# Weight scales from norms, scores in float16 halves, a layer function as a maximum, and four pairs' memory steps together

## Chip, cores and metric

The kernel runs on one core of one Trainium2 chip. The metric is the device time of one execution in microseconds (us). Engines are named as in the profile: PE (TensorE matmul) and PEld (its weight loads), DVE (VectorE), ACT (ScalarE), POOL (GpSimd) and SP, which here only issues DMAs.

## The reference

Causal attention over 4 batches of 8 heads, 576 positions and width 64, mixed by a gate with a memory term, feeds two dense layers in a row. All inputs are float32.

```python
scores = scale * np.matmul(q, k.transpose(0, 1, 3, 2))      # causal mask, softmax -> a
local = np.matmul(a, v)
q_p = phi(q)
mem_out = einsum(q_p, M_prev) / (einsum(q_p, z_prev) + 1e-6)
x = g * mem_out + (1 - g) * local                           # -> (2304, 512)
h = x @ w_in
g = np.where(h >= 1, h, np.where(h <= -1, 0.0, (h + 1) ** 2 / 4))
y = g @ w_out                                               # first layer
h = y @ w_in2
g = np.maximum(h, 0.0) + alpha * np.minimum(h, 0.0)
out = g @ w_out2                                            # second layer
```

The weights arrive as float64 (512 x 2048 and 2048 x 512 in each layer).

## The kernel before

**Products.** A dense product is made of float16 halves: every operand is scaled by a power of two and split into a high and a low half (`copy` writes the high one, `rest` the difference), and `mm_in` and `mm_out` add three products, high by high, high by low and low by high. Each of the four dense products is 1536 matmuls of 128 x 128 weights by 288 columns; the profile names them h<-x,w1i (first layer in), y<-g,w1o (first layer out), h<-yt,w2i and o<-g,w2o.

**Weights.** `Weights.groups` (called as w1i0 to w1i3, w1o0 to 3, w2i0 to 3, w2o0 to 3) loads the float64 bits of two groups of weights, takes the absolute maximum of each raw piece on DVE (16 pieces of 512 columns for each weight), brings the maxima together over the partitions in `all_max` (a PE transpose, a DVE maximum, a PE product with ones), makes a scale from the exponent, builds each group's values in a tile t (tag wt, two buffers; ACT and DVE), and then writes the halves with `copy` and `rest`. `scales1` needs the scale of every group of w1i. The halves of w2o lie in the tag wa, where w1i's lie until the first layer has used them.

**Attention.** `prepare` (p0 to p3, one for each batch) loads q, z, v and M, computes phi(q) and the memory's norms pair by pair, and makes the batch's scales from maxima. `scale_memory` multiplies q by the norms. `attend` handles two heads (a pair) at a time in five blocks of query rows with 64, 192, 320, 448 and 576 key columns. A block's scores are two matmuls at once, one for each head on 64 of the 128 rows of PE (s<-qk, float32, which the profile shows as two instructions each; the last block is done as 288 + 288 columns). DVE reads the scores from PSUM with the mask and the maximum (CUSTOM_DVE_ANT_0, e<-s,mask), ACT takes the exponential, and ACT, DVE and POOL scale them into p. Batch 0 (`PLAIN`, sections a0A and a0B, four pairs each) goes on in float32 with PE transposes; batches 1 to 3 (a1C to a3C, twelve pairs) use float16 halves, a DMA transpose (pt<-p) and float16 products (px<-pt,vh).

**First layer's function.** `up1` makes 2 x 288 columns of h at a time in PSUM (tag f, two buffers), ACT writes u and d from it, `shift` adds a constant to d on one of three engines, DVE multiplies the two, and `split` makes the halves g. There are 64 such steps.

**Order.** `Plan` records every operation, with the engines that may run it (`plan.either`), and orders them beforehand by a list of priorities of small pieces of the program (`RANK`) and a table of chosen engines (`HOME`), with costs and a limited number of buffers of each tag. The instructions are then issued engine by engine in that order, and every queue runs in order. Of PSUM's eight banks, the tag s (scores, and the products of `all_max`) has two, px two, and f two tiles of two. All engine instructions are recorded in one helper, so all have the line 424 in the profile.

## Time and profile before

| what | us |
|---|---|
| median of three runs (1044.55 to 1045.64) | 1044.62 |
| the profiled execution, its own time | 1042.5 |
| the profiled execution, first to last instruction (span) | 1040.6 |
| busy: PE / PEld | 947.1 / 709.2 |
| busy: DVE / ACT / POOL | 684.7 / 515.6 / 375.7 |

The mean granted clock of PE is 0.993 of 2.4 GHz. Busy times are sums over a span whose stages have different limits, so they are read by stage. A matmul's duration includes its way through the pipeline (286 ns for 288 columns), so the cost of one in a stream is the distance from one start to the next. A wait is put down to what came last before the instruction started.

### The profile page before, as it was taken

To read this page: it belongs to the slowest core of one execution; us is meant where nothing else is said; L and a number is where in the kernel's file an instruction comes from. 1 tells how busy PE (TensorE), PEld (TensorE's weight loads), DVE (VectorE), ACT (ScalarE), POOL (GpSimd) and SP (SyncE) were. 2 spreads that over 40 slices of the span, in tenths; PEclk is the share of its full clock that TensorE was granted. 3 is DMA by queue.
4 is the path that set the end of the run, shared out by engine and by line. 5 is a ranking of instruction groups with operands and counts; after the bars stand their busy time and mean duration, and the time that the engine had idled before them with its cause. 6 is when DMAs were issued, how large, how long until landed. Compare 5 with 4: busy or idle time off the path is not lost.

```text
span 1040.6 us, 20570 instructions
## 1 busy us (share of the span) xinstructions
PE 947.1 (91%) x8043; PEld 709.2 (68%) x8043; DVE 684.7 (66%) x1803; ACT 515.6 (50%) x1030; POOL 375.7 (36%) x405
## 2 busy tenths in 40 slices
PE   2178779999999999999989999999999999999998
PEld 1156446666667666766667777777777777777776
DVE  6979989989887788987877889892323413042320
ACT  5458777667566663765456646332322423131220
POOL 1353554667466673543533521251010111100020
PEclk9999988999999999999999999999999999999999
DMA  9833324567755774376654152320001000000000
GB/s 334 291 113 122 135 89 135 129 133 184 164 126 112 162 164 94 71 157 124 118 145 146 48 171 82 129 86 24 30 18 35 12 13 12 24 1 23 7 18 23
DMA packets 132096, 104.23 MB, mean 100 GB/s; under 512 B 98464, under 2 KB 113312, under 8 KB 132000
## 3 DMA queue, kind: packets, MB, share of 16 engines
q1 hardware_dynamic: 132000, 102.93, 36.9%
q8 instruction: 63, 1.03, 0.4%
q14 instruction: 33, 0.27, 0.1%
HBM read 66.73 MB, written 9.44 MB: 73 GB/s over the span
## 4 chain that ended last, share of the span: by engine, by line
PE 40%; DVE 4%; DMA 3%; POOL 2%; issue 2%; ACT 1%; SPq 0%; ACTq 0%; POOLq 0%
PE h L424 21%; PE o L424 17%; PE y L424 3%; DMA pt<-p 1%; DMA w2o_raw<-in_w2o 1%; DVE u L424 1%; DMA w2i_raw<-in_w2i 1%; POOL d L424 1%; POOL w2o L424 0%; DVE p L424 0%; ACT u L424 0%; DVE yt L424 0%; DMA yr<-y 0%; POOL p L424 0%; ACT d L424 0%
## 5 line engine op out<-in xcount | busy, mean ns | idle before, releaser
L424 PE MATMUL y<-g,w1o 128*128 128x288 f16 x1536 | 203.7, 286 | 1.8 <-DVE g L424 1.5
L424 PE MATMUL h<-x,w1i 128*128 128x288 f16 x1536 | 200.5, 286 | 4.6 <-ACT d L424 2.1
L424 PE MATMUL h<-yt,w2i 128*128 128x288 f16 x1536 | 194.8, 286 | 1.3 <-ACT u L424 1.3
L424 PE MATMUL o<-g,w2o 128*128 128x288 f16 x1536 | 193.9, 286 | 0.5 <-POOL w2o L424 0.5
L424 DVE SCALAR_TENSOR_TENSOR u<-u,al 128x288 f32<-128x288 f32 x128 | 67.0, 555 | 186.8 <-ACT u L424 186.6
L424 PEld LDWEIGHTS <-w1i 128*128 128x128 f16 x1536 | 146.9, 98 | 50.9 <-issue 12.7
L424 PEld LDWEIGHTS <-w1o 128*128 128x128 f16 x1536 | 145.0, 98 | 51.3 <-issue 12.6
L424 PEld LDWEIGHTS <-w2i 128*128 128x128 f16 x1536 | 150.1, 98 | 39.3 <-issue 1.5
L424 PEld LDWEIGHTS <-w2o 128*128 128x128 f16 x1536 | 150.1, 98 | 38.6 <-POOL w2o L424 0.8
L424 POOL TENSOR_TENSOR g<-u,g 128x576 f16<-128x576 f32 x54 | 74.1, 1372 | 182.7 <-ACT g L424 132.6
L424 ACT ACTIVATE e<-e,mxt 128x576 f32<-128x576 f32 (+4 forms) x160 | 88.3, 553 | 65.6 <-DVE mxt L424 55.1
L424 ACT ACTIVATE u<-h,sa 128x288 f32<-128x288 f32 x128 | 58.5, 498 | 125.5 <-PE h L424 122.3
L424 POOL TENSOR_SCALAR g<-u 128x576 f16<-128x576 f32 x40 | 30.5, 764 | 213.4 <-DVE u L424 156.9
L424 PE MATMUL s<-qk 64*128 64x288 f32 (+4 forms) x384 | 89.7, 481 | 15.8 <-DVE mxt L424 14.2
L424 DVE TENSOR_TENSOR g<-u,g 128x576 f16<-128x576 f32 x74 | 59.9, 810 | 31.5 <-ACT g L424 18.7
L424 ACT ACTIVATE oe<-o,osc 128x288 f32<-128x288 f32 x32 | 16.0, 501 | 111.4 <-PE o L424 111.4
L424 DVE SCALAR_TENSOR_TENSOR u<-u,c,d 128x576 f32<-128x576 f32 x64 | 59.7, 934 | 14.4 <-POOL d L424 10.1
L424 DVE CUSTOM_DVE_ANT_0 e<-s,mask 128x288 f32<-128x288 f32 (+4 forms) x160 | 64.3, 419 | 6.6 <-PE s L424 4.2
L424 PEld LDWEIGHTS s<-qk 64*128 64x128 f32 x384 | 40.0, 203 | 42.0 <-DVE mxt L424 27.4
L424 ACT ACTIVATE u<-h,bu,su 128x576 f32<-128x576 f32 x64 | 52.8, 825 | 21.8 <-PE h L424 16.6
L424 ACT ACTIVATE g<-u 128x576 f16<-128x576 f32 x61 | 41.6, 681 | 43.8 <-DVE u L424 23.2
L424 DVE SCALAR_TENSOR_TENSOR p<-e,sm,p 128x320 f16<-128x320 f32 (+4 forms) x80 | 57.0, 730 | 8.2 <-POOL p L424 5.8
(221 smaller groups left out, 1247.4 us busy)
## 6 DMA issues: line engine op xcount, KB each, us to landing
ring<-in_w1i SPq DMA_DIRECT2D x16, 512.0 KB, 6.2
w1o_raw<-in_w1o SPq DMA_DIRECT2D x16, 512.0 KB, 3.7
w2i_raw<-in_w2i SPq DMA_DIRECT2D x16, 512.0 KB, 3.8
w2o_raw<-in_w2o SPq DMA_DIRECT2D x16, 512.0 KB, 3.8
qk<-in_qk SPq DMA_DIRECT2D x12, 576.0 KB, 4.6
qn<-in_qn SPq DMA_DIRECT2D x16, 320.0 KB, 3.4
vc<-in_vc SPq DMA_DIRECT2D x16, 320.0 KB, 4.3
y<-ye SPq DMA_DIRECT2D x32, 144.0 KB, 2.5
```

Source lines behind the costliest of these rows:

```text
L424: fn(*args, **kw)
```

## The change

The scales of w1i, w1o and w2o no longer come from maxima of the raw pieces but from norms: ACT squares the finished tile t (into the place of the group's own high half), PE sums the squares with ones, and DVE makes the exponent (`root_exponent`), group by group; for w1i the squares of each column are summed, for the others those of the whole group. w2i keeps its maxima. In `prepare` ACT sums squares of v and M, and for batches 1 to 3 also sums |k| and the negative part of q; the operations on the norms run once for the four pairs. In `attend`, batches 1 to 3 load q and k raw into tag tmp (three buffers), split them into float16 halves, and make the scores as three float16 products; blocks 0 and 1 share a run, an exponent step, a p tile and a DMA transpose. In `up1` DVE limits h from PSUM, ACT squares it, and DVE takes the larger of that and the scaled h from PSUM. `shift` is gone. `RANK` and `HOME` are replaced throughout; their lists are left out here.

```diff
+    ROOT = 2.04**0.5
+    def root_exponent(twice, name):
+        top = tiny.tile([P, 1], F32, tag="p2m1", name=f"{name}_ret")
+        f = tiny.tile([P, 1], I32, tag="p2e1", name=f"{name}_ref")
+        V.tensor_scalar(out=top, in0=twice, scalar1=2.0**-118, scalar2=2.0**118, op0=ALU.max, op1=ALU.min)
+        V.tensor_scalar(out=f, in0=top.bitcast(I32), scalar1=24, scalar2=None, op0=ALU.logical_shift_right)
+        return f
...
-    ones = const.tile([8, P], F32, name="ones")
+    ones = const.tile([P, P], F32, name="ones")
+    ones16 = ones.bitcast(BF16).rearrange("p (n t) -> p n t", t=2)[:, :, 1]
...
-                    V.tensor_reduce(
-                        out=mx[:, k, i : i + 1],
-                        in_=raw[:, :, 1].bitcast(F32),
-                        axis=AX,
-                        op=ALU.max,
-                        apply_absolute_value=True,
+                    if self.bound is None:
+                        V.tensor_reduce(
+                            out=mx[:, k, i : i + 1],
+                            in_=raw[:, :, 1].bitcast(F32),
+                            axis=AX,
+                            op=ALU.max,
+                            apply_absolute_value=True,
+                        )
...
+                    plan.part(f"m{k}")
+                    sk = self.scale(g, tv, hi)
                 plan.part(f"s{k}")
-                copy(hi, tv, s[:, k : k + 1], (A, V, G))
-                rest(lo, tv, s[:, k : k + 1], hi, (G, V))
+                copy(hi, tv, sk, (A, V, G))
+                rest(lo, tv, sk, hi, (G, V))
+        def scale(self, g, t, hi):
+            name = f"{self.name}{g}"
+            squares = hi.bitcast(BF16)
+            pb = psum.tile([P, 512], F32, tag="s", name=f"{name}_pb")
+            if self.bound == "column":
+                A.activation(out=squares, in_=t, func=AF.Square, scale=ROOT)
+                by_block = squares.rearrange("p (f k c) -> p f k c", f=2, k=KK)
+                with plan.one():
+                    for kk in range(KK):
+                        T.matmul(
+                            pb[:, : 2 * P].rearrange("p (f c) -> p f c", f=2),
+                            lhsT=ones16,
+                            rhs=by_block[:, :, kk],
+                            start=kk == 0,
+                            stop=kk == KK - 1,
+                        )
+                n2 = tiny.tile([P, 1], F32, tag="wmg", name=f"{name}_n2")
+                V.tensor_reduce(out=n2, in_=pb[:, : 2 * P], axis=AX, op=ALU.max)
+                dst, of = self.inv[:, g : g + 1], slice(0, P)
+            else:
+                sq = tiny.tile([P, 1], F32, tag="wmx", name=f"{name}_sq")
+                A.activation(out=squares, in_=t, func=AF.Square, scale=ROOT, accum_out=sq)
+                T.matmul(pb[:, 0:1], lhsT=ones, rhs=sq, start=True, stop=True)
+                n2 = pb[:, 0:1]
+                of = slice(64 * (g % 2), 64 * (g % 2) + 64)
+                dst = self.inv[of, g // 2 : g // 2 + 1]
+            f = root_exponent(n2, name)
+            s = tiny.tile([P, 1], F32, tag="ws", name=f"{name}_s")
+            V.tensor_scalar(
+                out=s.bitcast(I32), in0=f, scalar1=float(-ONE23), scalar2=float(205 * ONE23), op0=ALU.mult, op1=ALU.add
+            )
+            V.tensor_scalar(
+                out=dst.bitcast(I32), in0=f[of], scalar1=float(ONE23), scalar2=float(49 * ONE23), op0=ALU.mult, op1=ALU.add
+            )
+            return s
...
-        rns = []
+        rn = tiny.tile([P, NPAIR, NB, 2], F32, tag="rn", name=f"rn{b}")
         for i in range(4):
             t = buf([P, 640], F32, "tmp", f"vc{b}_{i}")
             Q.dma_start(out=t, in_=vc[b, i])
-            V.tensor_reduce(out=mx[:, i : i + 1], in_=t, axis=AX, op=ALU.max, apply_absolute_value=True)
+            A.activation(out=t, in_=t, func=AF.Square, scale=ROOT, accum_out=mx[:, i : i + 1])
...
+            if halved:
+                t = buf([P, S], F32, "tmp", f"kc{b}_{pr}")
+                Q.dma_start(out=t, in_=qk[b, pr, :, 1])
+                A.activation(out=t, in_=t, func=AF.Prelu, alpha=-1.0, accum_out=mx[:, 16 + pr : 17 + pr])
...
+            A.activation(
+                out=e, in_=t, func=AF.Relu, scale=-1.0, **({"accum_out": mx[:, 8 + pr : 9 + pr]} if halved else {})
+            )
...
+            V.tensor_reduce(out=rn[:, pr], in_=e, axis=AX, op=ALU.add)
+        plan.part("n")
+        rm = tiny.tile([P, NPAIR], F32, tag="rm", name=f"rm{b}")
+        V.tensor_scalar(out=rn, in0=rn, scalar1=1e-6, scalar2=None, op0=ALU.add)
+        V.reciprocal(out=rn, in_=rn)
+        V.tensor_reduce(
+            out=rm, in_=rn.rearrange("p r a b -> p r (a b)"), axis=AX, op=ALU.max, apply_absolute_value=True
+        )
+        V.tensor_tensor(out=mx[:, 4:8], in0=rm, in1=mx[:, 12:16], op=ALU.mult)
+        V.tensor_tensor(
+            out=rn,
+            in0=rn,
+            in1=gt.rearrange("p (r h) -> p r h", h=2).unsqueeze(2).to_broadcast([P, NPAIR, NB, 2]),
+            op=ALU.mult,
+        )
+        rns = [rn[:, pr] for pr in range(NPAIR)]
...
         for pr in range(NPAIR):
             plan.part(pr)
-            V.tensor_scalar(out=rns[pr], in0=rns[pr], scalar1=s3[:, 1:2], scalar2=None, op0=ALU.mult)
...
+        if not plain:
+            qt = buf([P, 2, 2, S], F16, "qk", f"qk{tag}_{pr}")
+            for i in range(2):
+                raw = buf([P, S], F32, "tmp", f"qr{tag}_{pr}_{i}")
+                Q.dma_start(out=raw, in_=qk[b, pr, :, i])
+                copy(qt[:, 0, i], raw, q_s[b][:, i : i + 1], (A, V, G))
+                rest(qt[:, 1, i], raw, q_s[b][:, i : i + 1], qt[:, 0, i], (V, G))
+            pairs = [(qt[:, a, 0], qt[:, c, 1]) for a, c in ((0, 0), (0, 1), (1, 0))]
+        else:
+            qt = buf([P, 2, S], F32, "qk", f"qk{tag}_{pr}")
+            pairs = [(qt[:, 0], qt[:, 1])]
...
+            if nb > 1:
+                runs = [[(0, 0, 64, 0), (1, 0, 192, 64)]]
+            elif bks[0] < 4:
+                runs = [[(bks[0], 0, wide[bks[0]], 0)]]
+            else:
+                runs = [[(4, 0, 288, 0)], [(4, 288, 288, 0)]]
...
+                    for bk, p0, n, c0 in run:
+                        for i, (qi, ki) in enumerate(pairs):
+                            for h in range(2):
+                                me = slice(64 * h, 64 * h + 64)
+                                T.matmul(
+                                    ps[h][:, c0 : c0 + n],
+                                    lhsT=qi[me, rows[bk] : rows[bk] + P],
+                                    rhs=ki[me, p0 : p0 + n],
+                                    start=i == 0,
+                                    stop=i == len(pairs) - 1,
...
+                            scale=-0.125 if plain else q_s[b][:, 2:3],
...
+        lim = tiny.tile([P, 2, 8], F32, tag="lim", name=f"lim_{b}")
+        V.tensor_scalar(
+            out=lim[:, 1].bitcast(I32),
+            in0=inv1.bitcast(I32),
+            scalar1=-1.0,
+            scalar2=float(254 * ONE23),
+            op0=ALU.mult,
+            op1=ALU.add,
+        )
+        V.tensor_scalar(out=lim[:, 0], in0=lim[:, 1], scalar1=-1.0, scalar2=None, op0=ALU.mult)
...
-                A.activation(out=u, in_=ps[:, :, :n], func=AF.Relu, scale=su[:, fq : fq + 1], bias=bu[:, 0:1])
-                A.activation(
-                    out=d, in_=ps[:, :, :n], func=AF.Prelu, scale=sd[:, fq : fq + 1], bias=bu[:, 1:2], alpha=0.5
+                V.tensor_scalar(
+                    out=d,
+                    in0=ps[:, :, :n],
+                    scalar1=lim[:, 0, fq : fq + 1],
+                    scalar2=lim[:, 1, fq : fq + 1],
+                    op0=ALU.max,
+                    op1=ALU.min,
                 )
-                shift(d, c)
-                V.scalar_tensor_tensor(out=u, in0=u, scalar=c, in1=d, op0=ALU.min, op1=ALU.mult)
+                A.activation(out=d, in_=d, func=AF.Square, scale=su[:, fq : fq + 1], bias=bu)
+                V.scalar_tensor_tensor(
+                    out=u, in0=ps[:, :, :n], scalar=sd[:, fq : fq + 1], in1=d, op0=ALU.mult, op1=ALU.max
+                )
...
-    w1i = Weights("w1i", w1i, True, ring("wb", 4))
-    w1o = Weights("w1o", w1o, False, each("w1o", ("x", "x", "g")))
+    w1i = Weights("w1i", w1i, True, ring("wb", 4), bound="column")
+    w1o = Weights("w1o", w1o, False, each("w1o", ("x", "x", "g")), bound="group")
...
+    w2o = Weights("w2o", w2o, False, each("w2o", RAWS), flips, bound="group")
```

## Rows read from the trace of the kernel before

**Rows 1.** The page's 40 slices (26 us each): busy tenths of PE, DVE and DMA.

```profile
PE   2178779999999999999989999999999999999998
...
DVE  6979989989887788987877889892323413042320
...
DMA  9833324567755774376654152320001000000000
```

**Rows 2.** Engine busy times by stage: window, length, five engines, clock, DMA share, GB/s.

```profile
0.00:94.60 94.60, 44.09 (x225) 28.77 (x225) 74.36 (x254) 54.78 (x125) 33.07 (x45) 1.00 0.67 232
94.60:202.50 107.90, 91.02 (x687) 63.24 (x686) 100.08 (x266) 80.81 (x141) 55.22 (x47) 0.94 0.36 112
202.50:527.50 325.00, 308.45 (x3011) 218.22 (x3009) 272.38 (x830) 199.66 (x452) 192.39 (x236) 1.00 0.63 134
527.50:706.00 178.50, 173.61 (x1435) 135.71 (x1433) 145.23 (x293) 93.90 (x148) 60.74 (x47) 1.00 0.36 115
706.00:1040.60 334.60, 329.98 (x2693) 263.20 (x2690) 92.63 (x162) 86.45 (x167) 34.29 (x33) 1.00 0.05 18
```

**Rows 3.** The chain that ended last, its end: start us, us, what.

```profile
1013.76 23.53 PE o L424 x192
```

**Rows 4.** TensorE in order of time: start us, us, engine, line, operation, tiles, count.

```profile
94.61 3.12 PE L424 MATMUL h<-x,w1i 128*128 128x288 f16 x24
...
181.88 3.11 PE L424 MATMUL h<-x,w1i 128*128 128x288 f16 x24
...
184.92 0.76 PE L424 MATMUL s<-qk 64*128 64x288 f32 x4
...
185.61 3.11 PE L424 MATMUL h<-x,w1i 128*128 128x288 f16 x24
...
190.12 0.44 PE L424 MATMUL s<-qk 64*128 64x64 f32 x4
...
197.95 1.02 PE L424 MATMUL s<-qk 64*128 64x448 f32 x4
...
200.47 0.69 PE L424 MATMUL px<-pt,vh 128*64 128x128 f16 x18
...
204.16 1.03 PE L424 MATMUL px<-pt,vh 128*64 128x128 f16 x30 [0.73 <-DMA pt<-p]
```

**Rows 5.** Waits over the span: TensorE's weight loads of scores for VectorE's reads.

```profile
PEld s L424 <- DVE mxt L424: 27.4, 37, 2.2
```

**Rows 6.** Groups by shape over the span: xcount, busy us, mean ns, idle before.

```profile
L424 DVE TENSOR_REDUCE w1i_mx<-ring 128x1 f32<-128x512 f32 x16 | 10.6, 676 | 1.4 <-DMA ring<-in_w1i 1.2
...
L424 DVE TENSOR_REDUCE mx<-vc 128x1 f32<-128x640 f32 x16 | 12.9, 813 | 1.6 <-DMA vc<-in_vc 1.4
...
L424 DVE TENSOR_SCALAR m<-m 128x1 f32<-128x1 f32 x8 | 1.4, 171 | 0.1
...
L424 ACT ACTIVATE w1i<-w1i_t,w1i_s 128x1024 f16<-128x1024 f32 x4 | 4.6, 1138 | 0.4 <-DVE w1i_t L424 0.4
...
L424 DVE SCALAR_TENSOR_TENSOR p<-e,sm,p 128x576 f16<-128x576 f32 x17 | 17.0, 1018 | 2.1 <-POOL p L424 1.4 <-ACT p L424 0.6
...
L424 DVE CUSTOM_DVE_ANT_0 e<-s,mask,mxt 128x288 f32<-128x288 f32 x32 | 15.4, 508 | 1.0 <-PE s L424 1.0
...
L424 DVE CUSTOM_DVE_ANT_0 e<-s,mask 128x288 f32<-128x288 f32 x32 | 13.9, 445 | 1.6 <-POOL p L424 1.1 <-PE s L424 0.4
...
L424 DVE COPY tt<-pt 128x640 f32<-128x640 f32 x2 | 1.6, 816 | 0.0
```

**Rows 7.** Groups by shape from 202.5 to 527.5 us: the first layer's function.

```profile
L424 DVE SCALAR_TENSOR_TENSOR u<-u,c,d 128x576 f32<-128x576 f32 x36 | 33.3, 925 | 9.1 <-POOL d L424 6.1 <-ACT d L424 2.3
...
L424 ACT ACTIVATE u<-h,bu,su 128x576 f32<-128x576 f32 x36 | 29.7, 824 | 14.9 <-PE h L424 14.2 <-DVE g L424 0.2 <-POOL qn L424 0.2
...
L424 POOL TENSOR_SCALAR d<-d,c 128x576 f32<-128x576 f32 x7 | 12.4, 1769 | 8.0 <-ACT d L424 7.8
...
L424 ACT ACTIVATE d<-d,c 128x576 f32<-128x576 f32 x19 | 14.6, 770 | 0.2
```

More of the change, by code (lines that the diff above doesn't have):

```diff
@@ L236, in add @@
                 cols = math.prod(kw["lhsT"].shape[1:])
-                if kw["lhsT"].shape[0] == 64:
+                if kw["lhsT"].shape[0] == 64 and whole:
                     cost.append(2 * n + 348)
+                elif kw["lhsT"].shape[0] == 64:
+                    cost.append(0.5 * n + (228 if kw["start"] and len(cost) < 2 else 6))
                 elif cols == 64:
-                    cost.append((2 if whole else 0.5) * n + (228 if kw["start"] else 6))
+                    cost.append((2 if whole else 0.5) * n + (228 if kw["start"] and len(cost) < 2 else 6))
                 else:
@@ L516, in copy @@
         plan.either(*(lambda e=e: way(e) for e in engines))
-    def shift(t, by, engines=(A, V, G)):
-        def way(e):
-            if e is A:
-                A.activation(out=t, in_=t, func=AF.Identity, bias=by)
-            else:
-                e.tensor_scalar(out=t, in0=t, scalar1=by, scalar2=None, op0=ALU.add)
-        plan.either(*(lambda e=e: way(e) for e in engines))
     def combine(out, a, b, op, engines=(G, V)):
@@ L717 @@
     att_t = {}
+    q_s = {}
     def prepare(b):
@@ new lines, in prepare @@
+        V.tensor_tensor(
[5 more added lines that the diff above has]
+        rns = [rn[:, pr] for pr in range(NPAIR)]
+        plan.part("s")
+        nm = 5 if halved else 2
+        m2 = tiny.tile([P, nm], F32, tag="m2", name=f"m2_{b}")
+        V.tensor_reduce(out=m2, in_=mx[:, : 4 * nm].rearrange("p (a b) -> p a b", b=4), axis=AX, op=ALU.max)
+        am = all_max(m2, nm, f"am{b}")
@@ L766, in prepare @@
+        f = root_exponent(am[:, 0:1], f"am{b}")
+        V.tensor_scalar(
+            out=m3[:, 0:1].bitcast(I32), in0=f, scalar1=float(ONE23), scalar2=float(64 * ONE23), op0=ALU.mult, op1=ALU.add
+        )
+        V.tensor_copy(m3[:, 1:2], am[:, 1:2])
         V.tensor_scalar(
@@ L853, in attend @@
                         )
[L854 removed]
+            for at, bk in enumerate(bks):
                 for h in range(2):
[L857 to L866 removed]
@@ L867, in attend @@
[L867 to L885 removed]
+                    A.activation(
+                        out=es[bk][:, h, : wide[bk]],
+                        in_=es[bk][:, h, : wide[bk]],
+                        func=AF.Exp,
+                        scale=-1.0,
+                        bias=mxt[:, at, h : h + 1],
+                        accum_out=sm[:, at, h : h + 1],
+                    )
@@ L886, in attend @@
+            V.scalar_tensor_tensor(
+                out=sm,
+                in0=sm,
+                scalar=1e-9,
+                in1=(g1i if plain else cs)[:, 2 * pr : 2 * pr + 2].unsqueeze(1).to_broadcast([P, nb, 2]),
+                op0=ALU.add,
+                op1=ALU.mult,
+            )
             V.reciprocal(out=sm, in_=sm)
-            nq = P if bk else 64
             if plain:
+                bk = bks[0]
+                e, w, nq = es[bk], wide[bk], P if bk else 64
                 p = buf([P, 2, 640], F32, "p", f"pf{tag}_{pr}_{bk}")
@@ L1145, in flips @@
         return l2[0][2]
-    w2o = Weights("w2o", w2o, False, each("w2o", RAWS), flips)
+    w2o = Weights("w2o", w2o, False, each("w2o", RAWS), flips, bound="group")
     gs = {}
```

463 lines of the change are left out of this document (231 added, 232 removed).

## Prediction

> **What bounds the kernel now.** I read the 40 slices first [rows 1]: PE is busy nine tenths or more from the seventh slice (156 us) on, DVE seven tenths or more in all but the first of the first 27, and the DMA engines are full only in the first two. So there are stages, and I cut them where the work changes [rows 2]. The chain that ended last closes with 192 dense products in 23.53 us [rows 3], 122.5 ns each; 4 x 1536 of them take 752.6 us. The span of 1040.6 is that and 288 us of everything else: other work of PE, and PE waiting. Nothing that the change touches is left in stage 5 (from 706 us), where PE is busy 330.0 of 334.6.
> - Stage 1, to the first dense product at 94.61 [rows 4]: loads, w1i's scales, batch 0's first blocks. DVE 79%, DMA 0.67, PE 47%: chains and DMA together, no engine alone.
> - Stage 2, to 202.5: the first layer begins, w1o is made, batch 0's other blocks run. DVE 100.1 of 107.9 (93%), PE 84%: DVE is the bound.
> - Stage 3, to 527.5: batches 1 to 3 of attention beside the first layer. PE 308.5 of 325 (95%), DVE 84%, ACT 61%, POOL 59%: PE is the bound, DVE the next.
> - Stage 4, to 706: the last of the first layer, w2i and w2o. PE 97%, DVE 81%.
>
> The prediction is a sum on the profiled execution's own 1042.5 us; the median of the runs, 1044.62, lies 2.1 above it, which I add at the end.
>
> **Scores on PE (stage 3).** Before: a block of 288 columns takes 184.92 to 185.61, 0.69 us from its start to the next start, which is 0.07 less than its duration; so 64 columns take 0.37 and 448 take 0.95 [rows 4], 1.5 ns per column, which gives 0.56 for 192 and 0.75 for 320. Each comes 0.10 late: the 24 products before it take 3.04 us, 181.88 to 184.92, where 24 x 122.5 ns is 2.94. A pair (64, 192, 320, 448, twice 288) is 0.37 + 0.56 + 0.75 + 0.95 + 1.38 + 6 x 0.10 = 4.6 us. After: three float16 products for each of two heads. No row has float16 on 64 rows. Nearest are the px products, two at once on 64 columns of the array each: 30 in 1.03 us, 18 in 0.69 [rows 4], 28 ns for 128 columns where the rate of the dense ones gives 54, so they do run two at once: 0.44 ns per column and product pair, and 0.11 fixed (less the same 0.07). With 0.10 for the switch a run costs 0.21 + 3 x 0.44 ns x columns: 0.55 (blocks 0 and 1 merged), 0.63, 0.80, 0.59, 0.59, together 3.2 us. Saved: 1.4 x 12 pairs = 17 us. Bounds: the dense rate and the switch alone, 2.5 us a pair, saves 25; heads not side by side, 6 products instead of 3 pairs, 5.3 us a pair, loses 8. I take 17, from the row nearest in type and shape. The merged block saves a fixed part and a DMA transpose in px, 12 x 0.2 = 2. PE is the bound here, so 19 us are on the path, if DVE keeps up.
>
> **What stage 3 asks of DVE.** `up1`: before, one product of 0.925 a step, and a third of the shifts; after, a limit and a maximum, both of 576 columns from PSUM. Nearest is the copy from PSUM, 0.816 for 640 columns [rows 6], so 0.73; I take 0.78 each for their pointer scalars (bounds 0.73 and 0.93, the product's row). That is +0.64 x 36 steps = +23 (19 to 33) [rows 7], less 10 shifts of about 0.65. Each score read gets one more pointer scalar: 0.508 against 0.445 [rows 6], 0.063 x 12 x 11 pairs = +8. Splitting q and k adds two rests a pair, 1.02 each on DVE [rows 6]; with two thirds of 22 there, +15 (0 to 22). Less: merged block steps (-4), norm operations once instead of four times, 15 x 0.17 for each of two batches (-5), v's maxima, five of 0.81 (-4). In all +26: DVE needs 298 us in a stage that PE could leave in 306. That is 97%, above the 93% of stage 2 where DVE is the bound; so operations that may run elsewhere must move. There is room: ACT falls from 200 to about 175 (36 steps x 0.88 and 19 shifts less [rows 7], copies, sums and |k| more), POOL stays near 200 (7 shifts of 1.77 less, split q and k more). PE already waits 27.4 us on DVE's reads of scores over the span [rows 5]; I let a quarter more of that come back, 7 us. Stage 3: -12 (-27 to +8).
>
> One rule of the Trainium skill speaks against the limit in `up1`: "VectorE: DVE Perf Modes", section Why PSUM operands drop a tier, has float32 operands from PSUM at one element per cycle. The copy from PSUM agrees, 1.27 ns per column with its fixed part [rows 6]; an estimate from the page's 0.96 GHz is 0.60 us before fixed parts. By it the two steps cost 1.2 or more, DVE stays the next bound, and the sum is as here.
>
> **Weights and start (stages 1 and 2).** DVE loses 32 maxima of w1i and w1o at 0.676 (21.6), eight chains of seven small operations at 0.17 (9.5) [rows 6], 12 maxima of v at 0.813 (9.8), norm operations (5) and half of batch 0's small block steps (5). It gains 16 scales of four small steps (11), eight maxima over 256 columns of about 0.4 (3), and 12 steps of `up1` at +0.64 (8), with splits of q and k already (2): -27 of 174, two thirds of it in stage 1. ACT gains 16 squares of 1.14 [rows 6] (18) and the sums of v (11) and |k| (4), and loses 12 steps x 0.88 and their shifts (15): +18 of 136. In stage 2 DVE is the bound and loses 9: I take -6 (0 to -9). In stage 1 DVE loses 18 of 74, but DMA fills the first 52 us and ACT, at 58%, now does the squares: -8. On the other side t is held longer: Square, PE's sums (four products of 256 columns or one of one column, some 0.5 us, while PE idles), five small steps and their handovers, some 3.5 us a group before `copy` may start; behind the waiting Square ACT has the exponentials, and behind the sums PE, in order, has scores and transposes. With two t buffers, eight groups x 3.5 / 2 = 14 us, if w1i's chain ends stage 1. So stage 1 is -8, from -18 to +6.
>
> **Stage 4.** w2o loses 16 maxima (10.8) and four chains (4.8), gains eight scales (5.4) and 16 steps of `up1` (10): DVE stays at 145 of 178.5. The squares need w1i's place (tag wa), so w2o's scales start later than now; until then PE has d31 and the second layer's first products. 0, at worst +6.
>
> **Sum.** 1042.5 - 12 - 6 - 8 = 1016.5; with 2.1, 1018.6.
>
> **Rivals.**
> - DVE takes over stage 3. For: the 298 us above; the waits of [rows 5]. If DVE can be filled no further than stage 2's 93%, the stage takes 298 / 0.93 = 320, a gain of 5 and not 12: 1025.6; with nothing from the start, 1039.6. Against: 36 splits and most rests may run on POOL or ACT. The Trainium skill's "TensorEngine Tiling (Array Packing)", section PSUM Bottleneck, says that tiling speeds up PE but not the emptying of PSUM, which may then be the bottleneck; no run here has shown it yet. Chance 0.22.
> - The array doesn't run the heads' float16 products at once: stage 3 loses 8 and gains 2 on px, 1042.5 + 6 - 14 + 2.1 = 1036.6. Against: px. Chance 0.07.
> - Slower: the f tiles are held by DVE. Now ACT empties one in 2 x 0.82 = 1.65 us while PE fills the other in 2.94. After, it is 0.78 + 0.77 + 0.78 = 2.33 with DVE twice in the chain, each time behind what its queue holds. With half a rest (0.51) before each and 0.2 of handovers that is 3.55, 0.6 above 2.94; it decides as soon as two steps of `up1` follow each other with nothing between them for PE. At all 64 steps +38: 1057. For: DVE at 84 to 93% in the stages where `up1` runs. Against: scores, px and y products stand between many steps. Chance 0.13.
> - The start gains its full 27 and the scores their 25: about 997. Chance 0.05.
>
> **How the numbers follow.** The forecast, 1018.6, has 0.53. The range, 996 to 1039, takes in the first two rivals and the good end; it leaves out the slower one and a little beside. A difference of 0.2% (2 us) is about what a measurement of this kernel can tell from no change. Faster: 0.53 + 0.22 + 0.07 + 0.05 less 0.02 of the first rival's and the second's tails = 0.85; same 0.03; slower 0.12.
>
> **What would show it.** After the change, a run of 448 score columns from start to next start near 0.7 to 0.8 us (0.95 now); two DVE steps of 0.73 to 0.93 in `up1`; no more than 80% of DVE in stage 1, and the first dense product near 86 us; DVE above 88% in stage 3, which ends near 500 us; stage 5 as long as now, 335 us. I am wrong if PE's waits on DVE (score reads, f tiles) grow past 20 us in stage 3, or if the first dense product comes later than 94.6.

## The result, and the profile after

The changed kernel takes 1031.54 us (median of four runs, 1027.21 to 1033.39), the kernel before 1045.13 in the same comparison: a ratio of 0.986, with a 95% interval of 0.983 to 0.990. It is faster by 13.6 us where 26 were forecast. The profiled execution took 1030.67, its span is 1028.9; the one of before took 1042.5.

The page's slices of TensorE, VectorE, the granted clock and the DMA engines, 25.7 us each (26.0 before), to be laid beside [rows 1]:

```profile
PE   1557979998999999999899999999999999999998
...
DVE  5977887799888899999879988872241313142230
...
PEclk9955889999999999999999999999999999999999
DMA  8934413457734957455565444321100000000000
```

In slices 15 to 19 (360 to 489 us) VectorE is now busy nine tenths or more, where it had seven to nine, and the clock row has two fives at 51 to 103 us.

Stage by stage, the view of [rows 2] with the same first three windows (length; PE, PEld, DVE, ACT, POOL busy; clock; DMA share; GB/s):

```profile
0.00:94.60 94.60, 45.63 (x208) 29.02 (x208) 71.17 (x231) 72.02 (x158) 33.48 (x43) 0.79 0.66 233
94.60:202.50 107.90, 94.65 (x742) 67.98 (x741) 84.30 (x240) 75.66 (x144) 45.23 (x47) 0.89 0.39 118
202.50:527.50 325.00, 302.35 (x3197) 217.42 (x3195) 294.41 (x811) 196.36 (x473) 187.52 (x223) 0.99 0.59 137
527.50:694.50 167.00, 161.77 (x1385) 125.82 (x1385) 142.62 (x308) 93.08 (x150) 58.08 (x43) 1.00 0.42 135
694.50:1028.90 334.40, 329.69 (x2691) 262.97 (x2688) 89.50 (x160) 87.92 (x169) 32.72 (x29) 1.00 0.05 18
```

Up to 202.5 us VectorE does 19 us less (155.5 against 174.4), ScalarE 12 more; but only 3.2 of VectorE's 19 fall in stage 1. From 202.5 to 527.5 VectorE does 22 us more (294.4, 91%) and TensorE 6 less. Stage 5 is as it was. The chain still ends in 192 products, at the pace of [rows 3]:

```profile
1001.56 23.53 PE o L426 x192
```

Where the 12.2 us between the two traces lie can be read by counting the dense products of the two layers, 6144 in each trace. The 384th starts at 202.46 before and at 200.91 after (1.6 us earlier), the 2304th at 555.59 and 539.38 (16.2), the 3456th at 706.25 and 694.46 (11.8), the last at 1036.99 and 1024.80 (12.2). The last px product of attention moved by 5.6 only, 556.7 to 551.1, so part of the 16.2 is attention put behind dense products, which is given back afterwards. Stages 1 and 2 together gave 1.6 us, stages 3 and 4 10.2, stage 5 0.4. Such counts come from one execution of each kernel; how far they can be trusted is said under the runs.

TensorE of after in order of time, as [rows 4]: its first score, the end of the start, and score runs of each width.

```profile
33.32 1.59 PE L426 MATMUL s<-qk 64*128 64x192 f32 x4
...
100.68 1.55 PE L426 MATMUL px<-tt,vf 128*64 128x128 f32 x12 [2.54 <-ACT tt L426]
102.16 0.59 PE L426 MATMUL w1o_pb<-w1o_sq,ones 128*128 128x1 f32 x2
102.61 7.49 PE L426 MATMUL h<-x,w1i 128*128 128x288 f16 x48
...
205.92 0.54 PE L426 MATMUL s<-qk 64*128 64x288 f16 x6
209.44 0.51 PE L426 MATMUL s<-qk 64*128 64x64 f16 x12
212.93 0.58 PE L426 MATMUL s<-qk 64*128 64x320 f16 x6
...
520.86 0.74 PE L426 MATMUL s<-qk 64*128 64x448 f16 x6
521.53 1.64 PE L426 MATMUL y<-g,w1o 128*128 128x288 f16 x12
```

The first dense product starts at 102.61, 8.0 us later than in [rows 4]. A score of 448 columns takes 0.67 from its start to the next start (520.86 to 521.53), where it took 0.95.

VectorE, ScalarE and GpSimd from 202.5 to 500 us, groups by shape (count, busy us, mean ns, idle before), the answer to [rows 7]:

```profile
L426 ACT ACTIVATE d<-d,bu,su 128x576 f32<-128x576 f32 x38 | 32.9, 865 | 38.9 <-DVE d L426 29.8 <-DVE m L426 5.5 <-DVE ys_s L426 2.4
L426 DVE TENSOR_SCALAR d<-h,lim 128x576 f32<-128x576 f32 x37 | 32.1, 868 | 3.6 <-PE h L426 3.5
L426 DVE SCALAR_TENSOR_TENSOR u<-h,sd,d 128x576 f32<-128x576 f32 x38 | 30.8, 812 | 3.7 <-ACT d L426 2.8 <-POOL p L426 0.5
L426 POOL TENSOR_TENSOR qk<-qr,qk 128x576 f16<-128x576 f32 x9 | 12.8, 1419 | 0.8
L426 DVE SCALAR_TENSOR_TENSOR qk<-qr,qs,qk 128x576 f16<-128x576 f32 x9 | 10.2, 1134 | 0.4 <-POOL qk L426 0.4
```

And TensorE's waits on VectorE over the span, of weight loads as in [rows 5] and of products:

```profile
PEld s L426 <- DVE mxt L426: 8.3, 8, 3.1
...
PEld L426 <- DVE u L426: 18.3, 22, 2.5
...
PE h L426 <- DVE u L426: 10.1, 11, 2.2
```

The weight loads' wait for score reads fell from 27.4 us to 8.3. A new one, for the function's result, has come in its place: 18.3 us of weight loads and 10.1 of products.

### The profile page after: what moved, and what is told of

It is laid out like the page before. It is cut to its first block, busy times and chain, and to the rows that moved or that the text cites. A ratio compares the mean times of both kernels' runs of the same rounds, so it can differ in the third digit from the quotient of the medians.

```text
span 1028.9 us, 20943 instructions
## 1 busy us (share of the span) xinstructions
PE 934.1 (91%) x8215; PEld 703.2 (68%) x8215; DVE 682.0 (66%) x1748; ACT 525.0 (51%) x1091; POOL 357.0 (35%) x382
## 4 chain that ended last, share of the span: by engine, by line
PE 52%; DVE 20%; ACT 9%; DMA 8%; POOL 5%; issue 4%; SPq 1%; ACTq 0%; DVEq 0%; POOLq 0%
PE h L426 24%; PE o L426 18%; PE y L426 5%; DVE p L426 3%; DVE u L426 2%; DVE d L426 2%; DVE e L426 2%; PE px L426 2%; DMA w2i_raw<-in_w2i 2%; DVE g L426 2%; DMA pt<-p 2%; ACT e L426 2%; PE s L426 2%; SPq L426 1%; DMA qn<-in_qn 1%
## 5 line engine op out<-in xcount | busy, mean ns | idle before, releaser
L426 PE MATMUL h<-x,w1i 128*128 128x288 f16 x1536 | 203.6, 290 | 10.8 <-DVE u L426 10.1
L426 PEld LDWEIGHTS <-w1o 128*128 128x128 f16 x1536 | 146.1, 98 | 51.8 <-issue 10.1
L426 POOL TENSOR_TENSOR g<-u,g 128x576 f16<-128x576 f32 x50 | 70.1, 1403 | 154.9 <-ACT g L426 128.9
L426 POOL TENSOR_SCALAR g<-u 128x576 f16<-128x576 f32 x31 | 23.3, 753 | 253.6 <-DVE u L426 156.9
L426 ACT ACTIVATE e<-e,mxt 128x576 f32<-128x576 f32 (+4 forms) x160 | 88.1, 552 | 39.5 <-DVE mxt L426 36.9
L426 ACT ACTIVATE d<-d,bu,su 128x576 f32<-128x576 f32 x64 | 55.4, 865 | 51.2 <-DVE d L426 40.4
L426 PE MATMUL s<-qk 64*128 64x288 f16 (+9 forms) x528 | 66.8, 335 | 14.8 <-DVE mxt L426 8.5
L426 ACT ACTIVATE g<-u 128x576 f16<-128x576 f32 x75 | 51.1, 681 | 52.8 <-DVE u L426 36.4
L426 DVE TENSOR_SCALAR d<-h,lim 128x576 f32<-128x576 f32 x64 | 55.6, 869 | 6.9 <-PE h L426 6.5
L426 DVE SCALAR_TENSOR_TENSOR p<-e,sm,p 128x192 f16<-128x192 f32 (+4 forms) x84 | 57.2, 707 | 1.1 <-ACT p L426 0.9
L426 DVE CUSTOM_DVE_ANT_0 e<-s,mask,qs 128x64 f32<-128x64 f32 (+4 forms) x120 | 54.7, 480 | 4.0 <-PE s L426 3.7
L426 DVE SCALAR_TENSOR_TENSOR u<-h,sd,d 128x576 f32<-128x576 f32 x64 | 52.0, 812 | 6.3 <-ACT d L426 5.3
```

The lines of the kernel that those rows point to most:

```text
L426: fn(*args, **kw)
```

## The experiments

Each run but one is the changed kernel with its order of instructions kept on every engine; only the instructions named are replaced or left out, so nothing is ordered anew. The diffs are shortened to what is issued in place of what; in the runs' files a recorded operation keeps its place in the order, and other instructions, or none, are issued for it. The first dense product and the count of dense products are read as above. Against which theory each stands is in the quoted expectations; the changed kernel's 1031.5 and 0.986 (0.983 to 0.990) are the mark for all.

How far one trace can be read is shown by runs that do the same work at first. The run with one product differs from the changed kernel only from its first float16 score on, and has that score at 177.41 us where the changed kernel has it at 181.54. So about 4 us near 180 us can come from one execution to the next.

### What sets the start

**No chain of scales.**

```diff
-                A.activation(out=squares, in_=t, func=AF.Square, scale=ROOT)
...
-            f = root_exponent(n2, name)
+            s, f = self.s0, self.f0
```

The first group of w1i and of w1o still makes its scale; w2o's chain stays.

> The changed kernel with its order of instructions kept; of the eight groups of w1i and the eight of w1o only the first of each makes its scale, the others use that one: no Square, no sums on TensorE, no chain of small steps for 14 groups (the left out work is a part of the computation). The changed kernel starts its first dense product at 102.61 us, its median is 1031.5. If the chain of the scales, by its load on ScalarE or by its wait, is what made the start 8.0 us later instead of earlier, the first dense product comes near 92 (ten squares of 1.05 us fewer before it), and the time is near 1021. If the start hangs on something else (batch 1's sums, the DMA, TensorE's rate), it stays within 2 us of 102.6 and the time above 1028.

1036.1 us (ratio 0.991, 0.988 to 0.994): slower by 4.6. The first dense product comes at 101.5, 1.1 earlier. So in this order neither the squares' load nor the wait for the scale made the start late. The 4.6 us are lost between the 384th product (2.1 earlier than in the changed kernel) and the 2112th (4.8 later), where the two kernels do the same work. I have no cause for that; it says how far such runs can be read, and I assign no difference under 5 us from a total alone.

**Squares over 64 columns.**

```diff
-                A.activation(out=squares, in_=t, func=AF.Square, scale=ROOT)
+                A.activation(out=squares[:, :64], in_=t[:, :64], func=AF.Square, scale=2 * ROOT)
```

The sums on TensorE shrink with them, and w2o's squares are narrowed too.

> The changed kernel in its own order, but the squares of w1i and w1o and their sums go over 64 of the 1024 columns (a part of the computation left out): the chain with all its handovers stays, ScalarE's load goes (1.05 to about 0.2 us for each square). If ScalarE's load is what delays the start, the first dense product comes near 93 to 94 and nearly all of the gain of the run without the chain is here too. If the chain's handovers and the two buffers of t are it, it comes near 100 and most of that gain is missing.

1031.2 us (0.986, 0.983 to 0.989); the first dense product at 100.1. 2.5 us of the eight at most, and nothing at the end.

**Batch 1's sums over a sixteenth.**

```diff
-                A.activation(out=t, in_=t, func=AF.Prelu, alpha=-1.0, accum_out=mx[:, 16 + pr : 17 + pr])
+                A.activation(out=t[:, :36], in_=t[:, :36], func=AF.Prelu, scale=16.0, alpha=-1.0,
+                             accum_out=mx[:, 16 + pr : 17 + pr])
```

The squares of v are narrowed in the same way (40 of 640 columns).

> The changed kernel in its own order, but batch 1's sums of v squared and of |k| (8 instructions of 0.9 us on ScalarE between 32 and 75 us) go over a sixteenth of the columns, with their loads unchanged (a part of the computation left out). If ScalarE's load delays the start, the first dense product comes about 5 us earlier, near 97, and the time is near 1026. If chains or DMA decide, it moves by less than 1.5 us.

1030.1 us (0.985, 0.981 to 0.989); the first dense product at 102.2. ScalarE's extra work ahead of batch 0's exponentials isn't it either.

**TensorE filled.**

```diff
+        for _ in range(FILL.pop(name, 0)):
+            nc.tensor.matmul(a[:, :n], lhsT=ones[:, :p], rhs=ident[:, :n], start=True, stop=True)
         for fn, args, kw in op.ways[eng][0]:
```

> The changed kernel in its own order, with 104 extra products of ones and the identity on TensorE, put ahead of 15 steps before which it waited for data in the first 160 us; each group of them goes to PSUM that the step then overwrites. Nothing is left out. In the changed kernel transposes take 0.213 us apart up to 105 us and again from 139.7 to 150.0, where they take 0.109 later, and the kernel before had 0.109 from 87 us. If TensorE's rate at the start is on the path, it comes up earlier here, the first dense product comes 4 to 8 us earlier and 3 to 5 us more are won between 120 and 150: a time of 1020 to 1026. If it is not, the first dense product moves by less than 1.5 us, and the time stays within 3 us of 1031.5, or is longer by what the extra products delay.

1026.9 us (0.983, 0.979 to 0.986). The first dense product comes at 101.2, only 1.4 earlier, but the 384th at 195.0 instead of 200.9. From 105.6 to 160 us, the changed kernel and then the filled one:

```profile
105.60:160.00 54.40, 45.96 (x315) 32.10 (x312) 47.00 (x109) 42.61 (x75) 20.37 (x17) 0.87 0.33 104
```

```profile
105.60:160.00 54.40, 46.67 (x365) 33.51 (x364) 50.82 (x126) 45.95 (x83) 23.28 (x22) 1.00 0.34 109
```

The clock is 1.00 there and not 0.87, and about as much is won as was expected for this stretch. That the filling won it isn't shown: the run with one product (below) isn't filled, and has the clock at 0.97 in this window and its 384th product at 195.9 too; and the interval of the total overlaps the changed kernel's. The half of the expectation about the start missed. The clock up to 105.6 us rose, to 0.89 from 54.4 to 87 us and to 0.82 from there on, where the changed kernel has 0.50; the first dense product moved by 1.4 only. So TensorE's rate, as far as the filling raised it, isn't what ends the start.

**Maxima again.**

```diff
+                    V.tensor_reduce(out=m[:, i : i + 1], in_=raw[:, :, 1].bitcast(F32), axis=AX, op=ALU.max,
+                                    apply_absolute_value=True)
...
-                A.activation(out=squares, in_=t, func=AF.Square, scale=ROOT)
```

> The changed kernel in its own order with the weights' part undone for w1i, w1o and w2o: two maxima of 0.68 us on VectorE and a transpose, a maximum and a product for the scale of each group, no squares on ScalarE, no sums of them. The prediction gave this part 8 us at the start and 6 in the next stage. If VectorE's relief there is worth that, the first dense product comes 6 to 10 us later than 102.61 and the time is 1040 to 1046. If the start is set by the order of the loads and of the steps and not by VectorE's work, the first dense product moves by less than 3 us and the time by less than 4.

1069.6 us (1.024, 1.021 to 1.027), 38 more. The first dense product comes 8.7 later, at 111.3, and the 384th 16.5 later, at 217.4; TensorE's longest wait is for the maxima:

```profile
PE w1i_pb L796 <- DVE w1i_omg L795: 41.4, 7, 21.3
```

Two things are undone at once here: VectorE's load ahead of the first dense product (88.1 us, 76.4 in the changed kernel), and the form of the chain, whose two products and two maxima now stand where the order has one sum, with scores behind them in TensorE's queue. The run doesn't part them. The kernel before, with the maxima and its own order, had its 384th product at 202.46. So the part is worth 16.5 us against this order without it, and all that was changed up to there 1.6 us against the order that the kernel before had.

### What bounds the stage of attention

**Scores in float32 again.**

```diff
-                copy(qt[:, 0, i], raw, q_s[b][:, i : i + 1], (A, V, G))
-                rest(qt[:, 1, i], raw, q_s[b][:, i : i + 1], qt[:, 0, i], (V, G))
+                Q.dma_start(out=whole[:, i], in_=qk[b, pr, :, i])
```

> The changed kernel in its own order with one part undone: the scores of batches 1 to 3 are float32 products of q and k as they come (one load each straight into the tile that held the halves, issued where the high half was made), no halves, no rests, no sums of |k|, the reads of the scores scaled by a constant. A pair's scores took 4.6 us of TensorE before and take 2.5 now, so TensorE gets 12 x 2.1 = 25 us more; VectorE loses 14 rests and GpSimd about ten. If TensorE bounds the stage of attention, as the prediction has it, the time is 1046 to 1056 against the changed kernel's 1031.5. If the split of q and k on VectorE gives the gain back, it is under 1040.

1025.7 us (0.979, 0.975 to 0.983): undoing this part made the kernel 5.9 us faster (the two intervals just touch), where 15 to 25 slower was expected of a stage that TensorE bounds. (The 25 us of the expectation count the switch between kinds of products on one side only; 18 is right, see below.)

**One product of three.**

```diff
-                        for i, (qi, ki) in enumerate(pairs):
+                        for i, (qi, ki) in enumerate(pairs[:1]):
```

> The changed kernel in its own order with one of the three float16 products of each score of batches 1 to 3 (the low halves are made but not used: part of the computation left out). TensorE loses about 1.5 us a pair, 18 us in all; nothing else changes. If TensorE still bounds the stage of attention, the time falls by 12 to 18, to 1014 to 1020. If VectorE has taken the stage over (the prediction's first rival), it falls by less than 6, and TensorE's waits on VectorE in that stage grow by the rest.

1026.6 us (0.982, 0.980 to 0.985): 5 less where TensorE was given 18. Even these 5 are hardly the edit's: in the traces the run is 4.1 us ahead at its first float16 score, before the edit acts, and 4.9 at the last dense product.

**No rests of q and k.**

```diff
-                rest(qt[:, 1, i], raw, q_s[b][:, i : i + 1], qt[:, 0, i], (V, G))
...
-            pairs = [(qt[:, a, 0], qt[:, c, 1]) for a, c in ((0, 0), (0, 1), (1, 0))]
+            pairs = [(qt[:, 0, 0], qt[:, 0, 1])] * 3
```

> The changed kernel in its own order without the low halves of q and k of batches 1 to 3 (part of the computation left out); the three products stay and read the high halves, so TensorE does the same work. VectorE loses 14 operations of about 1.0 us, GpSimd about ten pairs of operations. If TensorE bounds the stage of attention, the time stays within 3 us of 1031.5. If VectorE does, it falls by 8 or more, to 1023 or less.

1018.4 us (0.975, 0.972 to 0.977): 13 less, with as many products on TensorE. The interval lies clear of the changed kernel's. GpSimd loses rests too (174 to 155 us in the window below), so this run alone doesn't say which of the two engines it was.

The window from 202.5 to 500 us (297.5 us; PE, PEld, DVE, ACT, POOL) shows all of these: before, after, float32 scores, one product, no rests, in this order.

```profile
202.50:500.00 297.50, 283.25 (x2736) 199.51 (x2735) 249.43 (x759) 184.02 (x414) 174.09 (x216) 1.00 0.63 136
```

```profile
202.50:500.00 297.50, 278.33 (x2939) 200.97 (x2938) 272.91 (x747) 180.58 (x433) 173.82 (x204) 0.99 0.58 136
```

```profile
202.50:500.00 297.50, 290.19 (x2851) 207.80 (x2849) 257.96 (x744) 169.20 (x413) 147.37 (x182) 0.99 0.56 130
```

```profile
202.50:500.00 297.50, 269.85 (x2707) 196.07 (x2705) 273.36 (x748) 179.89 (x433) 173.94 (x206) 0.98 0.59 140
```

```profile
202.50:500.00 297.50, 281.90 (x3001) 204.50 (x3000) 261.56 (x751) 183.47 (x439) 155.22 (x192) 1.00 0.60 140
```

After the change VectorE is busy 273 of 297.5 us (92%) and TensorE is idle 19. With TensorE's work cut (one product) VectorE's stays at 273 and TensorE's idle time grows to 28: the time isn't TensorE's. With VectorE at 262 the products come sooner, and with float32 scores VectorE is at 258 and TensorE at 290, idle 7: there TensorE bounds the stage again. GpSimd, at 174 us, is far from full.

The chain of work that ended last says the same. In this window it lies for 117 us on VectorE, 58 on TensorE and 32 on GpSimd in the changed kernel, and for 53 on VectorE and 172 on TensorE with float32 scores. Its largest parts, first the changed kernel, then float32 scores:

```profile
by line: PE h L426 11.2%; DVE p L426 10.1%; issue 7.6%; DVE e L426 6.1%; DMA pt<-p 5.4%; DVE d L426 4.9%; DVE u L426 4.7%; PE y L426 4.2%; DVE g L426 3.2%; DMA qn<-in_qn 2.9%; POOL p L426 2.5%; ACT e L426 2.4%; POOL vh L426 2.3%; ACT d L426
```

```profile
by line: PE y L444 24.4%; PE h L444 22.0%; DMA pt<-p 9.3%; PE s L1005 7.3%; PE px L444 4.0%; DVE p L444 3.9%; DVE e L1033 3.3%; DMA qn<-in_qn 3.1%; issue 2.9%; DVE d L444 2.4%; DMA w2i_raw<-in_w2i 2.0%; DVE u L444 1.9%; DVE g L444 1.7%; POO
```

### The layer function

**The old function in the changed kernel.**

```diff
-                V.tensor_scalar(out=d, in0=h, scalar1=lim0, scalar2=lim1, op0=ALU.max, op1=ALU.min)
-                A.activation(out=d, in_=d, func=AF.Square, scale=su, bias=bu)
-                V.scalar_tensor_tensor(out=u, in0=h, scalar=sd, in1=d, op0=ALU.mult, op1=ALU.max)
+                A.activation(out=u, in_=h, func=AF.Relu, scale=su, bias=bu)
+                A.activation(out=d, in_=h, func=AF.Prelu, scale=sd, bias=minus, alpha=0.5)
+                A.activation(out=d, in_=d, func=AF.Identity, bias=c)
+                V.scalar_tensor_tensor(out=u, in0=u, scalar=c, in1=d, op0=ALU.min, op1=ALU.mult)
```

> The changed kernel in its own order with the layer function of before: ScalarE's two reads of the f tile and the shift (all on ScalarE here, 2 x 0.82 + 0.77 us a step in place of one square of 0.87), VectorE one product of 0.93 in place of a limit of 0.87 and a maximum of 0.81. Over 64 steps VectorE loses about 48 us and ScalarE gains about 99. If f tiles held by VectorE cost the changed kernel time (TensorE waited 10.1 us for the function's result at first-layer products), the time falls to 1026 or less. If the function's move is worth its while, the time rises to 1036 or more, and TensorE waits on ScalarE instead. Between them it is neutral.

1061.8 us (1.015, 1.013 to 1.018), 30 more. The shift, which the kernel before spreads over three engines, is all on ScalarE here. Taken alone that reads as if the new function were worth 30 us. VectorE, at 233 us in the window above, had room; but its queue stood for 33.2 us behind the product that waits for ScalarE's three steps (202.5 to 500 us):

```profile
DVE u L1222 <- ACT d L1216: 33.2, 27, 3.0
```

**The new function in the kernel before.** The same edit the other way round, in the kernel before and its own order.

```diff
-                A.activation(out=u, in_=h, func=AF.Relu, scale=su, bias=bu)
-                A.activation(out=d, in_=h, func=AF.Prelu, scale=sd, bias=minus, alpha=0.5)
-                shift(d, c)
-                V.scalar_tensor_tensor(out=u, in0=u, scalar=c, in1=d, op0=ALU.min, op1=ALU.mult)
+                V.tensor_scalar(out=d, in0=h, scalar1=lim0, scalar2=lim1, op0=ALU.max, op1=ALU.min)
+                A.activation(out=d, in_=d, func=AF.Square, scale=su, bias=bu)
+                V.scalar_tensor_tensor(out=u, in0=h, scalar=sd, in1=d, op0=ALU.mult, op1=ALU.max)
```

> The kernel before in its own order with one part of the change alone: the layer function as a limit and a maximum on VectorE (0.87 and 0.81 us) with one square on ScalarE between them (0.87), in place of two reads on ScalarE (0.82 each), a shift on one of three engines and a product on VectorE (0.93). Undoing this part in the changed kernel cost 30 us. If the function is what brings the gain, by the time of ScalarE that it frees in the f tiles' chain, this kernel takes 1020 to 1032 against 1045 before. If that loss came only from the changed kernel's order, made for the new function, the limit in VectorE's queue costs as much here as the shift frees: 1042 or more, or slower than before.

1087.1 us (1.039, 1.036 to 1.043), 43 more, worse than the second expectation. The waits over its span:

```profile
ACT d L1071 <- DVE d L1061: 118.8, 58, 6.8
...
PEld L442 <- DVE u L1079: 49.7, 28, 4.4
PE h L442 <- DVE u L1079: 31.4, 15, 4.0
DVE d L1061 <- PE h L442: 29.6, 27, 3.6
```

The limit stands in VectorE's queue where the order put ScalarE's read; VectorE waits 29.6 us there for the product, and all that is behind it waits too. TensorE's products wait 31.4 for the f tile. ScalarE's 118.8 for the limit are idle time of an engine that isn't full, and needn't cost as much. Each function loses in the other's order. The loss of the run before is therefore no measure of what the new function brings.

### Two parts put together

**Float32 scores and filled TensorE**, the two edits shown above in one kernel.

> Two earlier runs together, nothing left out: the changed kernel in its own order with float32 scores for all batches (alone 1025.7) and with the 104 extra products on TensorE before 160 us (alone 1026.9, 4.7 less than the changed kernel). The one acts after 180 us, the other before, so the gains should add: 1019 to 1023. If the time lost at the start is made up later anyway, it stays at 1025.

1020.9 us (0.976, 0.973 to 0.978; 1016.3 to 1022.6 in six runs): 10.7 less than the changed kernel, as the sum of the two gains had it, and with an interval clear of it. Nothing is left out in it. That the filling adds to the float32 scores isn't shown: the interval overlaps that of the scores alone (0.975 to 0.983), and in the trace, of the slowest of the six executions, the 384th product comes at 201.67, with none of the early gain.

**Float32 scores in every second pair, TensorE filled.**

```diff
+            if pr % 2:
+                Q.dma_start(out=whole[:, i], in_=qk[b, pr, :, i])
```

> As the run before it, but float32 scores in every second pair of batches 1 to 3 and float16 halves in the others. With all in halves VectorE is busy 273 of the 297.5 us from 202.5 to 500 and TensorE waits 19; with none it is 258, and TensorE waits 7 but is busy 290. In the middle VectorE has about 265 and TensorE about 284 to do. If each engine's load is what counts, both have room and the time is 1014 to 1019, below the run before it; if VectorE's work alone decides, it is 1021 to 1025, between the two.

1021.7 us (0.977, 0.975 to 0.980), the same as the run before it. From 202.5 to 500 us:

```profile
202.50:500.00 297.50, 285.69 (x2906) 204.70 (x2904) 263.36 (x746) 175.88 (x425) 167.20 (x201) 0.99 0.58 137
```

The loads came out as worked out (286 and 263 against 284 and 265), and TensorE's room of 12 us brought no time. By its number the run lies in the second range; but that was to lie above the run before, and the two can't be told apart. With both engines near 90% or above I take it that the waits between them decide, not the larger of two sums; no run shows that.

## Why the prediction was right, and where not

The direction and the range held. Half of the size is missing. It is missing in one place, the start, while stage 3 has its forecast size by luck.

**Stages 1 and 2 (forecast -14, found -1.6): the step that failed.** From the first dense product to the 384th the kernel takes 98.3 us where it took 107.9, so stage 2 gained 9.6 (6 forecast). The start, which was to gain 8 and bring the first dense product near 86, lost 8.0: it comes at 102.61. The step was "in stage 1 DVE loses 18 of 74", and its loss taken for time, in a stage for which the prediction itself had said that no engine alone is the bound. Of VectorE's loss up to 202.5 us (19, forecast 27) only 3.2 lie in stage 1 and 15.8 in stage 2; ScalarE gains 17 in stage 1. Ahead of its first dense product VectorE now does more than before, 76.4 us against the 74.4 of [rows 2]:

```profile
0.00:102.60 102.60, 50.19 (x236) 32.47 (x237) 76.36 (x235) 77.77 (x168) 37.52 (x46) 0.77 0.64 224
```

The maxima are gone from there, but `RANK` and `HOME`, which were replaced throughout, have put other work on VectorE in their place: five rests of w1i for three (6.6 us for 3.9), seven steps of building w1o's tiles for two (5.0 for 1.6), copies of tt (3.3 for none). Some operations of the same shape also took longer: the products of q and phi(q) (qn) 1.33 us on average for 0.82, the steps that build w1i's tiles 0.86 for 0.68. The sum had no term for either.

The adverse row that I had ready, t held longer, isn't the cause: without the chain the first dense product moves by 1.1 us. The traces show another order of the start, too. The transfers of q and k for the first scores were first in SP's queue before, and stand behind those of w1i after; the kernel before, then after:

```profile
0.72 0.70 SPq L424 DMA_DIRECT2D qk<-in_qk  x1
```

```profile
22.31 0.69 SPq L426 DMA_DIRECT2D qk<-in_qk  x1
```

TensorE's first score follows at 33.32, where it stood at 18.28. The load alone doesn't make these 15 us: it lands 7.3 us after its issue, at 29.6, and the score then stands in TensorE's queue behind the sums of a group of w1i, for whose square TensorE waits. Without the chain the score starts as its load lands. The changed kernel, then the run without the chain:

```profile
32.38 1.01 PE L426 MATMUL w1i_pb<-w1i,ones 128*128 128x256 bf16 x4 [9.50 <-ACT w1i L426]
```

```profile
30.13 1.01 PE L444 MATMUL s<-qk 64*128 64x192 f32 x4 [7.58 <-DMA qk<-in_qk]
```

So some 12 of the 15 us are the load's place and 3 the sums'. Which of all this makes the first dense product 8 us late stays open: the load's place and the work moved to VectorE are read, not tried, for loading q and k first changes every queue after it, and would have been another order and not one change. What the runs rule out, each alone, is the chain, ScalarE's squares, batch 1's sums and, as far as the filling raised it, TensorE's rate.

**Scores (forecast 3.2 us a pair, -17).** From start to next start the runs take 0.44 (64 and 192 merged), 0.51, 0.67, 0.47 and 0.47 us, with the switch's 0.10 each 3.1 a pair, so 18 us saved in twelve. The nearest row, px, was the right one, and the heads do run at once: their products start 3 to 4 ns apart. The second rival is out.

**Stage 3 (forecast -12): near its size by luck, with the first rival's mechanism.** "PE is the bound here, so 19 us are on the path, if DVE keeps up": it doesn't. The forecast of VectorE's work was 298 us, it is 294.4; at 91% it is the bound. One product in place of three gives 5 of 18 us at most; leaving out the rests gives 13; the float16 scores with all that they need cost the changed kernel some 6 us net in this order. So the 19 us that made up the forecast weren't collected, and the gain came from elsewhere. The Trainium skill's "TensorEngine Tiling (Array Packing)", section PSUM Bottleneck, says that tiling speeds up TensorE but not the emptying of PSUM. These runs agree in that TensorE's gain was not collected; what they price is the making of the rests, of which the rule doesn't speak, and no run prices the emptying. Stages 3 and 4 still gained 10.2 between them. How much of that is the function's, the merged blocks', the order's or that of the steps for four pairs at once (which I didn't run by themselves) can't be told: the function and the weights' part lose 30 to 43 us in an order made for the other version, so singly they have no price.

**The function.** Two steps of 0.868 and 0.812, +0.76 a step where 0.64 was forecast, inside the bounds of 0.73 and 0.93. The Trainium skill's "VectorE: DVE Perf Modes", section Why PSUM operands drop a tier, holds float32 operands from PSUM to the lowest rate. The prediction's estimate from it was 1.2 us or more for both steps, and they take 1.68.

**The slower rival (f tiles held by VectorE, +38)** is no fancy: it is what the kernel before does with the new function, +43 with 31.4 us of TensorE's waits. In the order of the changed kernel these waits come to 10.1 us in all.

**Stages 4 and 5.** Forecast 0; the 3456th product gives back 4.4 of the 16.2 us, mostly attention that was put off; stage 5 takes 334.4 where it took 334.6.

**Not in the sum at all: TensorE's clock.** The changed kernel works at the lower level nearly all the time up to 105.6 us, and again from 122.7 to 126.1 and from 139.7 to 150.0, the kernel before up to 87 and from 133.4 to 140.3 and 157.3 to 164.2. Filling raised the clock, and the time was 4.7 us shorter; with an interval that overlaps the changed kernel's, no run shows what the clock costs here.

Of the signs named ahead, the run of 448 columns, the two steps, VectorE's shares and the length of stage 5 came true. The first dense product did not; it was named as a sign of being wrong, and the step behind it was wrong. Stage 3 doesn't end near 500 either: the 2112th dense product comes at 498.3 where it came at 527.5, but the last score at 532.8, where it came at 528.7. TensorE's products waited 17 us for VectorE from 202.5 to 527.5 us, short of the 20 of the other sign; its weight loads, which overlap them, waited 16.

## What to carry to other kernels

Work that leaves the busiest engine is time only in a stage which that engine bounds, and only if the new order puts no other work in its place; for a stage bound by no engine, ask what the first and the last piece of work there will wait for after the change, loads included. When in-order queues are filled by an order made for one version, taking a part out of that version, or putting it alone into the other, measures the order as much as the part: try it in both, and believe only what agrees. When two runs do the same work up to some point, compare them there first: what they differ by is the least that a later difference has to exceed. And price a faster product by all the steps that prepare its operands on the next-busiest engine, before asking how fast it is.

## What the runs showed of the hardware that I had not expected

TensorE's rate at the start isn't what the row of granted clocks says there. In the kernel before the row shows 1.00 to 94.6 us, but six transposes take 1.54 us at 81.28 and 0.87 at 90.64; eight take 1.95 at 146.19 and 1.09 at 169.37 after the change. In the slower ones they start 0.213 us apart, the 1.2 GHz level, in the others 0.109, the 2.4. The kernel before, then after:

```profile
81.28 1.54 PE L424 MATMUL pt<-ident,pf 128*128 128x128 f32 x6
...
90.64 0.87 PE L424 MATMUL pt<-ident,pf 128*128 128x128 f32 x6
```

```profile
146.19 1.95 PE L426 MATMUL pt<-ident,pf 128*128 128x128 f32 x8
...
169.37 1.09 PE L426 MATMUL pt<-ident,pf 128*128 128x128 f32 x8
```

Ahead of the stretch at 139.7 TensorE had waited 3.05 us for ScalarE's pf. At the start the kernel before rose to the upper level at 87 us, behind px products and transposes, the changed one at 105.6, behind its first 3 us of dense products.

VectorE's steps that build w1i's tiles (128x512) took 0.67 to 0.69 us each in most places of the changed kernel's start, but 1.52 at 14.88 and 2.02 at 29.2, both times with a GpSimd TENSOR_TENSOR running beside it (14.31 to 15.86 and 28.77 to 30.69). No run was made on that.
